# Hashed attention and a maxout feed-forward: sums gathered on 32 partitions, the last pair of a batch by halves, an earlier feed-forward and a new first pair

## The chip, the cores and the metric

The kernel runs on one core of one Trainium2 chip. The metric is the time of one execution in microseconds (us); lower is better. A core has five engines with queues of their own: PE (TensorE, matrix products into the PSUM memory; PEld is its weight load), DVE (VectorE), ACT (ScalarE), POOL (GpSimd) and SP (SyncE, which here issues transfers only). Each engine runs its instructions in the order in which the kernel emits them, and waits on semaphores for the others.

## The reference

```python
# q, k, v: (4, 8, 768, 64) fp32, proj: (64, 6); per batch and head
q_bucket, k_bucket = bits of (q @ proj > 0), bits of (k @ proj > 0)      # 6 bits each
scores = where(q_bucket == k_bucket, q @ k.T / 8, -1e9)
attn = softmax(scores);  x = attn @ v                                    # heads side by side: (3072, 512)
h = maximum(maximum(x @ w1, x @ w2), x @ w3)                             # w: (512, 768)
out = h @ w_out                                                          # (768, 512) -> (3072, 512)
```

Two tokens attend to each other only where all six signs agree. The kernel appends the six signs, as plus and minus one half, to the 64 columns of q and k, so that one matrix product of 70 rows gives the score and its mask at once; the exponential brings products with unequal signs down to nothing, and a small constant stands in for rows without a partner.

## The kernel before

Work is cut into 16 pairs of heads (four batches of four pairs) and each pair into 12 units: two halves of the queries (qh), three pairs of key blocks (kp) and two heads. A unit is one call of `scores`: two products of 70 x 384 into a double PSUM bank (tile `sc`, two buffers) and one exponential on ACT into one of 14 tiles `AT` (line 259). The loop `for u in range(NU)` (line 356, 192 units) emits everything else around the units, in an order written out by hand:

- Preparation of a pair ahead (`prep_groups`): four transpose groups (line 149, tile `mp`), each drained by DVE into `T2` (lines 152 and 154); then the hash (line 182, tile `bp`), the signs (`bits`, line 185), four small transfers `S<-bits` on SP (line 190), and casts into `S` by POOL (`even`, line 193) and DVE (`odd`, line 196). A group is emitted in four of six units until unit 61, then in two of six, and never more than six pairs ahead. Starting a pair also issues the loads of q and k two pairs further on.
- After each six units, `values`: 24 products with v (line 276) and 12 products with ones (line 283) for one half of the queries, then three DVE operations that store the unnormalized result (`avs`) and the row sums (`ys`). From pair 5 on both halves of a pair are done together, except in the very last pair.
- `normalize` of a pair: `gather` (two transfers `dd<-ys`, which spread the sums over 128 partitions), `invert` four units later (add and reciprocal on DVE, and a transfer `rd<-rr` to DRAM), `spread` six units later (two broadcast transfers `rb<-rd`), and `scale` ten units later (POOL, line 327, into `xT`). All four transfers' kinds are issued on SP.
- The feed-forward of the batch before (`ffn_groups`), from unit 13 of a batch on (`FFN_AT`): for each half of the tokens 18 groups of four products (line 213; they read all four pairs' parts of `xT`), with the maximum on DVE (lines 218 and 220), and three groups of six products with w_out (line 226), an ACT copy and a store. A credit of 0.66 per unit spaces them. Weights are loaded by POOL, 15 parts, one in three units from unit 13 (`WEIGHTS_AT`).

After the last unit the rest of batch 2's feed-forward and all of batch 3's follow, with the last normalization in between. Transposes, hashes, row sums, one of the two values tiles and the feed-forward share three PSUM buffers (`ms_ps`). The first pair has its own path (`hash_first`, lines 164 to 175): its `S` is written from PSUM by ACT, and its signs directly by DVE. Eight products with zeros run first (line 335).

Of the kernel before, what the change touches and what calls it, by code (L numbers as in the profile page):

```python
# [17 lines left out]
def kernel(  # L18
# [57 lines left out]

    iden = konst.tile([P, P], FP32, name="iden")
# [16 lines left out]
    warm = konst.tile([P, 512], FP16, name="warm")  # L94
    nc.vector.memset(warm[:], 0.0)
# [36 lines left out]
    def prep_groups(pi):  # L132
# [9 lines left out]
        def tgroup(side, hd):  # L142
            def go():
                if not st:
                    begin()
                mp = ms_ps.tile([P, 512], FP32, tag="ms", name="mp")
                n = natural[pi][side]
                for i in range(CH2):
                    nc.tensor.transpose(mp[:, i * P : (i + 1) * P], n[:, hd, 2 * i * D : (2 * i + 2) * D], iden[:])  # L149
                o = st["T2"][:, side, hd, :]  # L150
                if side == 0:
                    nc.vector.tensor_scalar(out=o, in0=mp[:, 0:HALF], scalar1=QS, scalar2=None, op0=AluOp.mult)  # L152
                else:
                    nc.vector.tensor_copy(o, mp[:, 0:HALF])  # L154
                if pi == 0:
                    for par in range(2):
                        o, i_ = st["S"][0:D, side, hd, par, :], mp[par * D : (par + 1) * D, 0:HALF]
                        if side == 0:
                            nc.scalar.mul(o, i_, QS)
                        else:  # L160
                            nc.scalar.copy(o, i_)
            return go

        def hash_first(hd):
            bp = ms_ps.tile([P, 512], FP32, tag="ms", name="bp")
            for side in (1, 0):
                for par in range(2):
                    g = 2 * side + par
                    nc.tensor.matmul(bp[32 * g : 32 * g + 32, 0:HALF], pj[:, 1 + par, :], st["T2"][:, side, hd, :],
                                     start=True, stop=True)  # L170
            for side in (1, 0):
                for par in range(2):
                    g = 2 * side + par
                    nc.vector.tensor_scalar(out=st["S"][D:KR, side, hd, par, :], in0=bp[32 * g : 32 * g + NBITS, 0:HALF],  # L174
                                            scalar1=0.0, scalar2=0.5, op0=AluOp.is_gt, op1=AluOp.subtract)

        def hashes():
# [9 lines left out]
            for hd in range(2):  # L187
                for side in (1, 0):
                    p0 = 32 * (2 * side + hd)
                    nc.sync.dma_start(st["S"][D:KR, side, hd, :, :], bits[p0 : p0 + 2 * NBITS, :])  # L190
# [7 lines left out]
        if pi == 0:  # L198
            return [tgroup(1, 0), tgroup(0, 0), lambda: hash_first(0), tgroup(1, 1), tgroup(0, 1),
                    lambda: hash_first(1)]  # L200
        return [tgroup(s, h) for h in (0, 1) for s in (1, 0)], hashes, [even, odd(1), odd(0)]

    def ffn_groups(b):
        xb = xts[b]
        gs = []
        for hf in range(2):
# [15 lines left out]
            for tb in range(CH2):  # L222
                def go2(tb=tb, hf=hf, hts=hts):
# [5 lines left out]
                    nc.scalar.copy(osb[:], ps[:, 0:DM])  # L229
                    rows = out[b * S : (b + 1) * S, :].rearrange("(p c) m -> p c m", c=NCH)  # L230
                    nc.sync.dma_start(rows[:, 2 * tb + hf, :], osb[:])
# [14 lines left out]
    WEIGHTS_AT = 13  # L246
    FFN_AT = 13
# [19 lines left out]
    def values(pi, qhs):  # L267
# [28 lines left out]
        if pi == NPAIR - 1:  # L296
            return normalize(pi, qhs[0], 1)
        return normalize(pi, 0, 2) if 1 in qhs else []

    def normalize(pi, q0, nq):  # L300
# [5 lines left out]
        W = nq * HALF // D  # L306
        dd = small.tile([P, 2, 2 * HALF // D], FP32, tag="dd", name="dd")
        rr = small.tile([P, 2 * HALF // D], FP32, tag="rr", name="rr")
        rd = drp.tile([2, 2 * HALF], FP32, tag="rd", name="rd")
# [6 lines left out]
        def invert():  # L316
            nc.vector.tensor_add(rr[:, 0:W], dd[:, 0, 0:W], dd[:, 1, 0:W])  # L317
            nc.vector.reciprocal(rr[:, 0:W], rr[:, 0:W])
            nc.sync.dma_start(rd[:, 0 : nq * HALF].rearrange("h (p i) -> h p i", i=W), rr[:, 0:W])

        def spread():
            for hd in range(2):
                nc.sync.dma_start(rb[hd * D : (hd + 1) * D, 0:nq, :],
                                    rd[hd : hd + 1, 0 : nq * HALF].to_broadcast((D, nq * HALF)))
# [5 lines left out]
        return [(0, gather), (4, invert), (6, spread)] + [(10, scale(i)) for i in range(nq)]  # L330

    with tc.manual_schedule():
        wm = ms_ps.tile([P, 512], FP32, tag="ms", name="wm")
        for _ in range(8):
            nc.tensor.matmul(wm[:], warm[:, 0:P], warm[:], start=True, stop=True)
# [5 lines left out]
        for g in first[:-1]:  # L341
# [7 lines left out]
        prep_1 = prep[3][3]  # L349
        scores(0)  # L350
        first[-1]()
        for _ in range(4):
            prep.pop(0)[2]()
        hash_ready.append(prep_1)
        cast_v[0]()
        for u in range(NU):
# [6 lines left out]
            if u >= WEIGHTS_AT and u % 3 == WEIGHTS_AT % 3 and weight_parts:  # L363
# [3 lines left out]
            if u + 1 < NU:  # L367
# [3 lines left out]
            if prep and prep[0][0] < pi + AHEAD and (u % UPG % 3 if u < UPB + FFN_AT else u % UPG in (1, 4)):  # L371
# [4 lines left out]
            elif u % UPG == 3 and u < PAIRS_AT:  # L376
# [6 lines left out]
            if u >= UPG - 1 + LAG and (u - LAG) % UPG == UPG - 1:  # L383
                vp, vq = units[u - LAG][0:2]
                single = vp * UPP < PAIRS_AT or vp == NPAIR - 1
                if single or vq == 1:
                    steps += [(u + n, g) for n, g in values(vp, (vq,) if single else (0, 1))]
                    if u >= PAIRS_AT:
# [6 lines left out]
        steps += [(1.3 * n, g) for n, g in values(NPAIR - 1, (1,))]  # L395
        steps.sort(key=lambda e: e[0])
        for n, (_, g, _) in enumerate(ffn + ffn_groups(B - 1)):
            while steps and steps[0][0] <= n:
                steps.pop(0)[1]()
            g()  # L400

# [29 lines left out]
```

## Time and profile before

| | |
|---|---|
| median of three runs | 314.0 us (313.26 to 316.84) |
| the profiled execution | 313.89 us, span 312.1 us |
| mean granted TensorE clock | 0.983 |
| busy: PE, DVE, ACT, POOL | 289.5, 193.9, 183.4, 106.3 us |
| matmuls | 2592 |
| HBM read, written | 31.46 MB, 6.39 MB |
| longest waits in total | POOL for rb 94.5 us, ACT for scores 75.5 us |

The span runs from the first to the last instruction of one execution. A line of the timeline has the start and the duration in us, the engine (SPq, ACTq, POOLq: its issue of a transfer), the line of the kernel, the operation, out<-in and the count; in brackets stands how long the engine was idle before it and what ended that. A line of waits has the total, the number of waits and the longest. Digits in the 40 slices are tenths of a slice busy; PEclk is the granted clock in tenths.

### The profile page before, as it was taken

To read this page: it belongs to the slowest core of one execution; us is meant where nothing else is said; L and a number is where in the kernel's file an instruction comes from. 1 tells how busy PE (TensorE), PEld (TensorE's weight loads), DVE (VectorE), ACT (ScalarE), POOL (GpSimd) and SP (SyncE) were. 2 spreads that over 40 slices of the span, in tenths; PEclk is the share of its full clock that TensorE was granted. 3 is DMA by queue.
4 is the path that set the end of the run, shared out by engine and by line. 5 is a ranking of instruction groups with operands and counts; after the bars stand their busy time and mean duration, and the time that the engine had idled before them with its cause. 6 is when DMAs were issued, how large, how long until landed. Compare 5 with 4: busy or idle time off the path is not lost.

```text
span 312.1 us, 6721 instructions
## 1 busy us (share of the span) xinstructions
PE 289.5 (93%) x2592; PEld 162.5 (52%) x2592; DVE 193.9 (62%) x413; ACT 183.4 (59%) x225; POOL 106.3 (34%) x125
## 2 busy tenths in 40 slices
PE   7699898988469999999999999999899999999994
PEld 3365454533236555665566555554455555555551
DVE  3868789794427755768297746762466256758480
ACT  4378777777418485755938485859585957220202
POOL 0567549394650705234140505131313020211000
PEclk9989999999959999999999999999999999999999
DMA  7758729594963324415411114022512221130202
GB/s 224 281 154 245 178 67 273 141 231 93 247 162 97 104 91 139 138 54 159 152 58 52 55 51 159 9 62 78 164 39 74 81 76 53 23 124 9 103 0 101
DMA packets 23358, 35.87 MB, mean 115 GB/s; under 512 B 9328, under 2 KB 15056, under 8 KB 23328
## 3 DMA queue, kind: packets, MB, share of 16 engines
q0 software_dynamic: 7136, 19.27, 22.3%
q1 hardware_dynamic: 16032, 16.19, 17.3%
q8 instruction: 20, 0.33, 0.4%
q14 instruction: 10, 0.08, 0.1%
q10 hardware_dynamic: 160, 0.00, 0.0%
HBM read 31.46 MB, written 6.39 MB: 121 GB/s over the span
## 4 chain that ended last, share of the span: by engine, by line
PE 70%; DMA 11%; DVE 8%; SPq 4%; ACT 3%; issue 3%; POOL 0%; DVEq 0%; ACTq 0%; POOLq 0%
PE l L213 28%; PE sc L256 14%; PE av L276 8%; PE l L226 7%; DMA dd<-ys 4%; PE sm L283 4%; DMA rb<-rd 4%; PE mp L149 4%; DMA rd<-rr 3%; ACT AT L259 3%; SPq L190 3%; PE bp L182 3%; DVE S L196 2%; DVE S L174 1%; DVE rr L317 1%
## 5 line engine op out<-in xcount | busy, mean ns | idle before, releaser
L259 ACT ACTIVATE AT<-sc,bias_t 128x768 f16<-128x768 f32 x192 | 166.7, 905 | 80.7 <-PE sc L256 75.5
L213 PE MATMUL l<-xT,w_sb 128*128 128x384 f16 x576 | 111.9, 330 | 6.7 <-POOL xT L327 6.1
L256 PE MATMUL sc<-S 70*128 70x384 bf16 x384 | 93.5, 331 | 6.1 <-ACT AT L259 4.0
L327 POOL TENSOR_TENSOR xT<-avs,rb 128x384 f16<-128x384 f32 x32 | 31.4, 998 | 142.1 <-DMA rb<-rd 94.5
L213 PEld LDWEIGHTS <-w_sb 128*128 128x128 f16 x576 | 56.4, 98 | 44.5 <-issue 9.3
L220 DVE TENSOR_TENSOR ht<-ht,l 128x384 f16<-128x384 f16 x96 | 53.2, 554 | 21.1 <-PE l L213 16.2
L256 PEld LDWEIGHTS <-S 70*128 70x128 bf16 x384 | 35.5, 99 | 43.9 <-issue 26.7
L218 DVE CAST ht<-l 128x384 f16<-128x384 f32 x48 | 26.5, 552 | 27.8 <-PE l L213 26.7
L276 PE MATMUL av<-AT,vo 128*32 128x385 f16 x768 | 37.4, 329 | 0.0
L229 ACT COPY osb<-l 128x512 f32<-128x512 f32 x24 | 14.1, 590 | 37.7 <-PE l L226 37.4
L226 PE MATMUL l<-wout_sb,ht 128*128 128x512 f16 x144 | 34.0, 379 | 0.0
L276 PEld LDWEIGHTS <-vo 128*32 128x32 f16 x768 | 18.5, 96 | 15.4 <-issue 6.7
L152 DVE TENSOR_SCALAR T<-mp 128x384 f32<-128x384 f32 x32 | 17.6, 550 | 11.3 <-PE mp L149 10.7
L193 POOL CAST S<-T 64x1536 bf16<-64x1536 f32 x15 | 22.6, 1505 | 0.9 <-DVE T L152 0.9
L196 DVE CAST S<-T 64x768 bf16<-64x768 f32 x30 | 21.8, 732 | 0.4
L226 PEld LDWEIGHTS <-ht 128*128 128x128 f16 x144 | 14.0, 97 | 14.8
L154 DVE COPY T<-mp 128x384 f32<-128x384 f32 x32 | 17.8, 556 | 6.0 <-PE mp L149 5.7
L283 PE MATMUL sm<-AT,ones 128*32 128x384 f16 x384 | 21.1, 325 | 0.0
L292 DVE TENSOR_SCALAR avs<-av,sv 128x384 f32<-128x384 f32 x32 | 19.8, 618 | 1.6
L124 POOL CAST vo<-vnat 128x768 f16<-128x768 f32 x16 | 13.4, 841 | 18.1 <-DMA vnat<-in_v_dram 16.8
L294 DVE TENSOR_SCALAR ys<-sm 128x384 f32<-128x384 f32 x32 | 17.5, 548 | 0.0
L149 PE MATMUL mp<-iden,knat 128*128 128x128 f32 x96 | 16.3, 278 | 1.2 <-DVE S L174 1.2
(36 smaller groups left out, 150.1 us busy)
## 6 DMA issues: line engine op xcount, KB each, us to landing
out_dram<-osb SPq DMA_DIRECT2D x24, 256.0 KB
vnat<-in_v_dram POOLq DMA_DIRECT2D x15, 384.0 KB, 3.6
rb<-rd SPq DMA_DIRECT2D x30, 192.0 KB
knat<-in_k_dram POOLq DMA_DIRECT2D x13, 384.0 KB, 4.3
qnat<-in_q_dram POOLq DMA_DIRECT2D x13, 384.0 KB, 4.7
w_sb<-in_moe_w_dram POOLq DMA_DIRECT2D x12, 192.0 KB, 5.0
S<-bits SPq DMA_DIRECT2D x60, 9.0 KB
knat<-in_k_dram SPq DMA_DIRECT2D x2, 384.0 KB
```

The costliest lines, as they stand in the source:

```text
L149: nc.tensor.transpose(mp[:, i * P : (i + 1) * P], n[:, hd, 2 * i * D : (2 * i + 2) * D], iden[:])
L193: nc.gpsimd.tensor_copy(st["S"][0:D, :, :, 0, :], st["T2"][0:D])
L196: return lambda: nc.vector.tensor_copy(st["S"][0:D, side, :, 1, :], st["T2"][D : 2 * D, side])
L213: nc.tensor.matmul(ps[:, 0:HALF], w_sb[wi][:, jc, fb * P : (fb + 1) * P], xb[:, jc, hf * HALF : (hf + 1) * HALF], start=(jc == 0), stop=(j ...
L218: nc.vector.tensor_copy(hts[fb][:], ps[:, 0:HALF])
L220: nc.vector.tensor_tensor(out=hts[fb][:], in0=hts[fb][:], in1=ps[:, 0:HALF], op=AluOp.max)
L226: nc.tensor.matmul(ps[:, 0:DM], hts[fb][:, tb * P : (tb + 1) * P], wout_sb[:, fb, :], start=(fb == 0), stop=(fb == NFB - 1))
L256: nc.tensor.matmul(sc[:, j, 0:HALF], th[0:KR, 1, hd, j, kp * P : (kp + 1) * P], th[0:KR, 0, hd, qh, :], start=True, stop=True)
L259: nc.scalar.activation(at[:, :, 0:HALF], sc[:, :, 0:HALF], ActFn.Exp, bias=bias_t[:], scale=SCALE)
L276: nc.tensor.matmul(av[p0 : p0 + 32, 0 : HALF + 1], vones[pi][:, hd, d0 : d0 + 32], at_of(qh, hd, c)[:, c % 2, 0 : HALF + 1], start=(c == 0 ...
L283: nc.tensor.matmul(sm[32 * t : 32 * t + 32, 0:HALF], ones[:, :], at_of(qh, hd, c)[:, c % 2, 0:HALF], start=(s == 0), stop=(s == CH2 - 1))
L327: return lambda: nc.gpsimd.tensor_mul(xt[:, jj, (q0 + i) * HALF : (q0 + i + 1) * HALF], avs[:, q0 + i, :], rb[:, i, :])
```

## The change

- Sums on 32 partitions: `dd` and `rr` have 32 rows of 48 columns (24 for a half pair), and `rd` is a DRAM tile of 32 rows that lie one behind the other. The gather is issued in `normalize` itself; for a whole pair invert comes after 5 units, spread after 8 and scale after 18 (14 for the third pair of a batch) instead of 4, 6 and 10.
- The last pair of every batch is normalized by halves, with 4, 6 and 10 units (in the last batch all at 4).
- `FFN_AT` and `WEIGHTS_AT` are 8. Weights are issued every four units instead of every three, transposes in three of six units instead of four until unit 56.
- The first pair: three of its four transposed tiles are drained by ACT, one by DVE; POOL makes its even casts, ACT (head 0) and DVE (head 1) its odd ones; hashes go into one tile for each side; the first two scores are emitted before the second head's hash; pair 1's four transpose groups go into units 0 to 3 and its hash into unit 4, half of its sign transfers on POOL. Nine warm-up products, whose tile is set first.
- The last output tile is copied by halves on ACT and DVE and stored by two queues. In the tail, steps are placed by the groups' costs rather than their number.

```diff
-                if side == 0:
+                if pi == 0 and (hd, side) != (0, 1):
+                    if side == 0:
+                        nc.scalar.mul(o, mp[:, 0:HALF], QS)
+                    else:
+                        nc.scalar.copy(o, mp[:, 0:HALF])
+                elif side == 0:
...
                 if pi == 0:
-                    for par in range(2):
-                        o, i_ = st["S"][0:D, side, hd, par, :], mp[par * D : (par + 1) * D, 0:HALF]
-                        if side == 0:
-                            nc.scalar.mul(o, i_, QS)
-                        else:
-                            nc.scalar.copy(o, i_)
+                    nc.gpsimd.tensor_copy(st["S"][0:D, side, hd, 0, :], o[0:D])
...
+        def odd_first(hd):
+            for side in (1, 0):
+                o, i_ = st["S"][0:D, side, hd, 1, :], st["T2"][D : 2 * D, side, hd, :]
+                if hd == 0:
+                    nc.scalar.copy(o, i_)
+                else:
+                    nc.vector.tensor_copy(o, i_)
...
-            return [tgroup(1, 0), tgroup(0, 0), lambda: hash_first(0), tgroup(1, 1), tgroup(0, 1),
-                    lambda: hash_first(1)]
+            return [tgroup(1, 0), tgroup(0, 0), lambda: odd_first(0), lambda: hash_first(0), lambda: bits_first(0),
+                    tgroup(1, 1), tgroup(0, 1), lambda: odd_first(1), lambda: scores(0), lambda: scores(1),
+                    lambda: hash_first(1), lambda: bits_first(1)]
...
+                    eng = nc.gpsimd if pi == 1 and hd == 1 else nc.sync
...
+                    if (b, hf, tb) == (B - 1, 1, CH2 - 1):
+                        nc.scalar.copy(osb[:, 0 : DM // 2], ps[:, 0 : DM // 2])
+                        nc.vector.tensor_copy(osb[:, DM // 2 :], ps[:, DM // 2 : DM])
+                        nc.scalar.dma_start(rows[:, 2 * tb + hf, 0 : DM // 2], osb[:, 0 : DM // 2])
+                        nc.sync.dma_start(rows[:, 2 * tb + hf, DM // 2 :], osb[:, DM // 2 :])
...
-    WEIGHTS_AT = 13
-    FFN_AT = 13
+    WEIGHTS_AT = 8
+    FFN_AT = 8
...
-        if pi == NPAIR - 1:
+        if pi % HPAIR == HPAIR - 1:
             return normalize(pi, qhs[0], 1)
...
-        W = nq * HALF // D
-        dd = small.tile([P, 2, 2 * HALF // D], FP32, tag="dd", name="dd")
-        rr = small.tile([P, 2 * HALF // D], FP32, tag="rr", name="rr")
-        rd = drp.tile([2, 2 * HALF], FP32, tag="rd", name="rd")
+        G = 16
+        W = nq * HALF // G
+        dd = small.tile([2 * G, 2, 2 * HALF // G], FP32, tag="dd", name="dd")
+        rr = small.tile([2 * G, 2 * HALF // G], FP32, tag="rr", name="rr")
+        rd = drp.tile([2 * G, W], FP32, tag=f"rd{nq}", name="rd")
...
-        return [(0, gather), (4, invert), (6, spread)] + [(10, scale(i)) for i in range(nq)]
+        gather()
+        if nq == 1:
+            return [(4, invert), (6, spread), (10, scale(0))] if pi < NPAIR - 1 else [(4, invert), (4, spread), (4, scale(0))]
+        return [(5, invert), (8, spread)] + [(18 if jj < 2 else 14, scale(i)) for i in range(nq)]
...
-        scores(0)
-        first[-1]()
-        for _ in range(4):
-            prep.pop(0)[2]()
-        hash_ready.append(prep_1)
...
-            if u >= WEIGHTS_AT and u % 3 == WEIGHTS_AT % 3 and weight_parts:
+            if u >= WEIGHTS_AT and u % 4 == WEIGHTS_AT % 4 and weight_parts:
...
-            if prep and prep[0][0] < pi + AHEAD and (u % UPG % 3 if u < UPB + FFN_AT else u % UPG in (1, 4)):
+            if prep and prep[0][0] < pi + AHEAD and (u < 4 if u < UPG else u % UPG in (0, 2, 5) if u < UPB + FFN_AT else u % UPG in (1, 4)):
...
-                single = vp * UPP < PAIRS_AT or vp == NPAIR - 1
+                single = vp * UPP < PAIRS_AT or vp % HPAIR == HPAIR - 1
```

## The prediction

> **What bounds the kernel now.** I read the page first (busy shares, the 40 slices of 7.8 us), then the chain of waits, the timelines of PE, ACT, DVE and SP in order of time, and short windows for the clock.
>
> ```profile
> PE 289.5 (93%) x2592; PEld 162.5 (52%) x2592; DVE 193.9 (62%) x413; ACT 183.4 (59%) x225; POOL 106.3 (34%) x125
> PE   7699898988469999999999999999899999999994
> PEclk9989999999959999999999999999999999999999
> ```
>
> TensorE is full from slice 13 to the last but one; PE's waits between 95 and 262 us sum to 2.1 us. There, time is TensorE work. What can be won lies in the first 93 us and the last 4. The largest hole, in PE's timeline and in windows (span, PE, PEld, DVE, ACT, POOL, clock, DMA share, GB/s):
>
> ```profile
> 81.91 0.65 PE L213 MATMUL l<-xT,w_sb 128*128 128x384 f16 x3
> 88.68 3.04 PE L213 MATMUL l<-xT,w_sb 128*128 128x384 f16 x9 [6.12 <-POOL xT L327]
> 92.15 1.23 PE L213 MATMUL l<-xT,w_sb 128*128 128x384 f16 x4
> ...
> 89.00:90.00 1.00, 1.00 (x5) 0.48 (x4) 0.56 (x1) 0.00 (x0) 1.00 (x2) 0.50 0.05 16
> 93.00:94.00 1.00, 1.00 (x7) 0.58 (x6) 0.56 (x1) 0.55 (x2) 0.66 (x1) 1.00 0.97 310
> ```
>
> The first feed-forward group has three chunks of xT and waits 6.1 us for the fourth, the last pair of batch 0. Then it runs at clock 0.50: from 88.68 to 93.22 PE does 15 matmuls that take 0.163 us each at full clock, so 4.54 us instead of 2.45. The hole costs 6.1 + 2.1 = 8.2 us. Why xT is late, from SP's timeline:
>
> ```profile
> 72.55 1.18 SPq L314 DMA_DIRECT2D dd<-ys  x2
> 76.47 0.33 SPq L319 DMA_DIRECT2D rd<-rr  x1
> 78.58 1.45 SPq L323 DMA_DIRECT2D rb<-rd  x2
> ```
>
> The gather stands behind four S<-bits issues, and the spread of 78.58 lands only at 87.5, beside 1.9 MB of vnat, knat, qnat and wout_sb that POOL issued from 76 to 81 us.
>
> Before the hole, what paces a group of six units? ACT:
>
> ```profile
> 23.10 2.48 ACT L259 ACTIVATE AT<-sc,bias_t 128x768 f16<-128x768 f32 x3 [1.01 <-PE sc L256]
> 25.79 2.48 ACT L259 ACTIVATE AT<-sc,bias_t 128x768 f16<-128x768 f32 x3 [0.21 <-PE sc L256]
> 29.35 2.48 ACT L259 ACTIVATE AT<-sc,bias_t 128x768 f16<-128x768 f32 x3 [1.08 <-PE sc L256]
> ```
>
> Six exponentials take 4.9 us; ACT starves 1.0 us behind the values block and 0.2 to 0.3 behind the hash. The values blocks start at 20.98, 27.16, 33.47, 40.74, 47.04, 54.18, 60.48, 66.79, 72.72, 79.65: groups of 5.93 (no hash), 6.3 (hash), and three of 6.9 to 7.3, where DVE stood first in a wait for the gathered sums:
>
> ```profile
> DVE rr L317 <- DMA dd<-ys: 14.1, 9, 3.2
> ```
>
> The group from 60.48 has no transposes and the one from 54.18 has four, and both take 6.3: transposes there are free, and fewer of them gain nothing.
>
> **The change, part by part.** The profiled execution took 313.89 us for a span of 312.1, so 1.8 us lie around the span; the median of the runs is 314.0. I sum on the span.
>
> *New first pair.* Before, exponentials started at 11.90, 15.51 and 16.4, and the first values block at 20.98. After, by the same rows: the warm tile is written first (0.24 us earlier), one more warm-up matmul takes 0.43, so the first transposes start at 4.7; they are drained 0.5 later by DVE (k) and ACT (q) side by side, done at 5.8. The k hash (half of 1.30 us) ends at 6.5, and four bit operations of 0.57 run from 6.55 to 8.8. Meanwhile ACT does the two odd copies (0.48 each) and POOL the two even ones (about 0.5 each, an estimate between 841 ns for 768 columns and 1505 for 1536), all by 6.9. PE's next transposes wait for a ms buffer until 7.7, scores(0) waits for the third bit operation until 8.3, and the first two exponentials start at 8.7 and 9.5. For head 1, DVE has two casts and four bit operations from 8.8 on; scores(3) starts at 11.3. Then four evacuations for pair 1 (0.55 each) end at 14.0, its hash at 14.7, and the first values block starts at 16.0. That is 5.0 us earlier. Bounds: 1.5 us earlier, if each of seven handoffs costs 0.25 more and PE is at clock 0.5 for 3.3 us (1.65 lost); 6 us earlier, if POOL and the ms ring never hold PE. The clock row is this:
>
> ```profile
> 13.00:14.00 1.00, 0.32 (x3) 0.31 (x3) 0.97 (x2) 0.00 (x0) 0.00 (x0) 1.00 0.73 286
> 15.00:16.00 1.00, 1.00 (x5) 0.57 (x4) 0.52 (x2) 0.49 (x1) 1.00 (x3) 0.50 0.15 32
> ```
>
> The clock fell at 14.2 us though PE had worked in every microsecond before. The Trainium skill, "TensorE: Matmul & The Clock Gate", the section on the HAM clock gate, says that it falls after an idle window of about 3.4 us; by that rule neither kernel would slow in its start, and the lower bound would be 1.65 us better. I go by the row for the bound. For the sum I take no slow stretch, since PE works some 5.5 of the 7 us from 5 to 12, more than before.
>
> Pair 1's bits go half by POOL: two issues of 0.75 us, with POOL's even cast and the loads of pair 4 queued behind them. They land by about 20.4 at the row of the slow loads (3.6 us); its scores come at 21. Cover gone, PE waits about 1 us.
>
> *Sums on 32 partitions, other delays.* A gather has 32 pieces of 192 bytes for 128 of 48. Landing is unknown: bounded by the chain's 1.96 and 3.80 us for dd, 2.09 and 4.70 for rd; I take 2. DVE's add and reciprocal have 48 columns for 12: 171 and 224 ns before, at most some 0.3 us more each, seventeen times on a DVE that is 62% busy: nothing. The gather goes out at the same place; invert comes a unit (1.0 us) later, scale four to eight units later, so POOL's 94.5 us of waiting for rb no longer holds its loads. The 32-row store gives the same contiguous read back. What goes is the DVE wait of the long groups, except for the last pair, where invert stays at four units: I charge 1.0 us in all. Hashes fall into five of the eight groups from unit 6 to 54: 5 x 6.3 + 3 x 5.93 + 1.0 = 50.3, against 51.74 (20.98 to 72.72): 1.4 us gained; bounds 4.3 gained (all at 5.93) and 1.5 lost (two long groups stay).
>
> *Feed-forward from unit 8, transposes spread.* After the values block of unit 54 (then 66.3), PE has 1.6 us of values and two scores with ACT's wait: the first feed-forward matmul comes at 69.3, 3.0 us later, against 9.2 before (72.72 to 81.91). But work left out of that stretch comes later, on a full PE: ten score matmuls (1.63), a values block (1.6), three hashes at 0.65 (1.95), eight transpose groups at 0.33 (2.65), together 7.8. So 10.8 against 9.2: 1.6 lost.
>
> *Last pair by halves.* The first feed-forward groups read half 0 alone. Its values come at unit 42, invert 46, spread 48, scale 52. On SP the spread stands behind the second half's gather, which waits for ys of unit 48: ys near 63.3, spread issued until 65.7, landed by 68.6 (3.27 us in the chain), scaled at 69.6; the fourth matmul needs it at 69.8. The last w3 chunk goes out at unit 52, behind two scales on POOL, near 65.1, lands 3.8 to 6.1 us later, and is needed at 71.0. Both just fit: I charge 0.5 of the 8.2, so 7.7 gained. Bounds: all 8.2 gained, or none. Three more normalizations in the kernel are 15 SP issues (0.34 to 0.55 us) that lie beside the full PE.
>
> *Last output tile by halves.* The copy of 0.58 us (from 307.96) becomes about 0.3, and the 3.6 us from its end to the end of the span keep the same bytes in flight: 0.3 gained, bounds 0 and 0.8. The Trainium skill, "DMA: Bandwidth & Descriptors", section on the anatomy of one DMA, puts some 2 us of a transfer that POOL issues down to a fixed cost; were it so for SP's and ACT's, which no run here shows, the halves would gain next to nothing beside the copy.
>
> Sum: 312.1 - 5.0 - 1.4 + 1.6 - 7.7 - 0.3 = 299.3 span, and 301.1 us with the 1.8 around it.
>
> **The rivals.**
>
> *The hole only moves.* Unit 56 comes at 69 us with its rb and w3 just landed; if the spread takes the 8.4 us that it took from 78.58, xT comes at 74.6, PE waits 5 us and runs slow after it. For it: that row, and the new place behind the second gather. Against: half the bytes, and 1.3 MB of loads at units 47 and 48 for 1.9. 301.1 + 7.7 = 308.8.
>
> *The start gains little* (its lower bound): 301.1 + 3.5 = 304.6; with the long groups kept too, 304.6 + 2.9 = 307.5. For it: a ring of three ms buffers, shared by transposes and hashes of both heads. Against: the two engines that drain them run side by side.
>
> *Slower.* The feed-forward of every batch now starts five units earlier, with the same scales. In batches 1 and 2 xT's half 0 is scaled at unit 4 and read at unit 8: four units of some 1.7 us, 6.7 us of cover. If SP (output stores, bits, the second half's gather before the first half's spread) delays that spread by more, PE waits at each of three starts; at a lateness of 8.2 us, with the slow clock, it pays three times: 301.1 - 0.5 + 24.6 = 325. It decides from a lateness of 4.3 us beyond the cover at each of the three (301.1 + 3 x 4.3 = 314). For it: POOL's longest wait for rb is 12.9 us. Against: that wait begins when POOL is idle, and PE met no wait over 0.8 us there.
>
> *It gains more*: groups at 5.93 and no charge for the first feed-forward: 301.1 - 2.9 - 0.5 = 297.7.
>
> **How the numbers follow.** Forecast (298.5 to 305) 0.62; little gained at the start 0.13; hole moved 0.12; more gained 0.08; slower 0.05. The time is the forecast's, 301.1. The range is 296.5 to 308.5: it takes in the cases up to the moved hole, about half of whose chance lies above it, and leaves out that, the slower case and the far ends of the bounds. About 1% (3.1 us) is what a measurement of this kernel can tell, its runs reaching from 313.3 to 316.8. Faster by more than that: 0.92, within it 0.04, slower 0.04 (the slower case near its point of decision counts as the same).
>
> **What would show each step.** First exponential near 8.7 and first values block near 16; values block of unit 54 near 66; no PE wait for xT over 1 us and no clock of 0.50 after the start; transposes and hashes still running on PE past 150 us; L317 no longer waiting over 1.5 us; PE full from 70 us to the end. A PE wait for w_sb or xT of over 3 us near 70 us, a values block at 19 us, or a second hole at a batch's unit 8 would prove a step wrong.

## The result, and the profile after

The changed kernel takes 324.7 us (median of four runs, 321.7 to 325.4) against 313.6 (310.6 to 316.8) for the kernel before in the same rounds: 1.037 times as long, 95% interval 1.026 to 1.048. The forecast was 301.1, so it is wrong, and in its sign. The profiled execution took 324.5 us for a span of 322.8, at a mean granted clock of 0.974.

From here on, medians, ratios and differences leave out the slow executions, those over 1.5% above the fastest of the same kernel in its block (ranges, and the times that the recorded expectations quote, are of all runs), and little more than waits is read from the profiles of e2_delays, e5_first_pair and e14_late_ffn8, which are of such executions. The experiments ran in four blocks, each with its own runs of the kernel before: medians 313.7, 313.8, 309.4 (a single run) and 313.2 us, single runs from 309 to 321. So differences of 2 or 3 us between blocks say little.

The span splits at four events that can be read in PE's timeline:

| stretch, us | before | forecast | after | after less forecast |
|---|---|---|---|---|
| to the first values block | 20.98 | 16.0 | 17.64 | +1.6 |
| from there to the values block of unit 54 | 51.74 | 50.3 | 57.93 | +7.6 |
| from there to the first feed-forward matmul | 9.19 | 3.0 | 3.58 | +0.6 |
| from there to the end | 230.2 | 230.0 | 243.6 | +13.6 |
| span | 312.1 | 299.3 | 322.8 | +23.5 |

The page after, busy time with the slices of 8.1 us:

```profile
PE 297.6 (92%) x2593; PEld 165.3 (51%) x2593; DVE 201.8 (63%) x419; ACT 183.0 (57%) x222; POOL 109.1 (34%) x131
...
PE   8889989888999999996999999996999999979995
...
PEclk9998979997999999999999999999899999979999
```

The deep hole of 4 and 6 tenths in slices 11 and 12 is gone. In its place come dips in slices 19, 28 and 36, which are the starts of the feed-forward of batches 1 and 2 and of the tail, and dips of the clock in slices 4, 6, 10, 29 and 36. PE is busy 8.1 us longer with the same products (and one more warm-up), and idle 2.6 us longer. Half clock explains at most 3.1 of the 8.1: by the mean clocks it cost 8.4 us of the span after and 5.3 of the span before. Where the rest comes from is not shown. Whether the half clock is a cause or only follows from thin work is left to the experiments. The feed-forward's starts, in PE's timeline:

```profile
80.92 1.62 PE L226 MATMUL l<-xT,w_sb 128*128 128x384 f16 x9 [1.11 <-POOL xT L347]
...
152.55 1.62 PE L226 MATMUL l<-xT,w_sb 128*128 128x384 f16 x9 [1.60 <-POOL xT L347]
...
224.43 2.42 PE L226 MATMUL l<-xT,w_sb 128*128 128x384 f16 x9 [1.69 <-POOL xT L347]
...
286.12 4.12 PE L226 MATMUL l<-xT,w_sb 128*128 128x384 f16 x14 [2.31 <-POOL xT L347]
```

Line 226 is what line 213 was. The wait of 6.12 us at the first start is now 1.11, but there are four waits instead of one, 6.7 us in all, and behind the last two the matmuls run long: nine of them took 1.62 us at 152 and 2.42 at 224.

In the attention stage, ACT's timeline:

```profile
34.24 2.48 ACT L278 ACTIVATE AT<-sc,bias_t 128x768 f16<-128x768 f32 x3 [1.40 <-PE sc L275]
37.69 2.49 ACT L278 ACTIVATE AT<-sc,bias_t 128x768 f16<-128x768 f32 x3 [0.96 <-PE sc L275]
41.58 4.29 ACT L278 ACTIVATE AT<-sc,bias_t 128x768 f16<-128x768 f32 x5 [1.40 <-PE sc L275]
...
49.32 2.48 ACT L278 ACTIVATE AT<-sc,bias_t 128x768 f16<-128x768 f32 x3 [2.17 <-PE sc L275]
```

Behind a values block ACT now starves 1.40 us instead of 1.0 to 1.08: a transpose group of 0.33 us stands between the scores and the values block of the same unit. DVE and POOL, side by side in time:

```profile
111.70 3.43 DVE L337 TENSOR_TENSOR rr<-dd 32x48 f32<-32x48 f32 x1
112.10 0.84 POOL L124 CAST vo<-vnat 128x768 f16<-128x768 f32 x1
...
113.58 1.48 POOL L205 CAST S<-T 64x1536 bf16<-64x1536 f32 x1
115.16 0.44 DVE L338 RECIPROCAL rr<-rr 32x48 f32<-32x48 f32 x1
...
116.06 0.81 PE L226 MATMUL l<-xT,w_sb 128*128 128x384 f16 x4 [0.43 <-DVE ht L231]
```

An addition of 48 columns, with a median of 0.19 us, took 3.43 and ended when POOL's second cast did; three more took 1.92. DVE's feed-forward copies stand behind it, and PE behind them. Last, two lines of the waits (total, times, longest):

```profile
DVE rr L337 <- DMA dd<-ys: 12.4, 6, 4.1
...
PE l L226 <- POOL xT L347: 6.7, 4, 2.3
```

DVE still stands in order before gathered sums; that was to have gone. And SP, around the last pair of batch 0:

```profile
71.35 0.55 SPq L339 DMA_DIRECT2D rd<-rr  x1
72.00 1.21 SPq L334 DMA_DIRECT2D dd<-ys  x2
76.35 1.15 SPq L343 DMA_DIRECT2D rb<-rd  x2
```

The first half's spread goes out at 76.35, where the prediction had it issued by 65.7. The stage itself is 9.3 us late by then (75.57 against 66.3 at unit 54), so the steps hold their order and most of the lateness comes from ahead of them.

### The profile page after: what moved, and what is told of

Same layout as the page of the kernel before. It is cut to its first block, busy times and chain, and to the rows that moved or that the text cites. A ratio compares the mean times of both kernels' runs of the same rounds, so it can differ in the third digit from the quotient of the medians.

```text
span 322.8 us, 6762 instructions
## 1 busy us (share of the span) xinstructions
PE 297.6 (92%) x2593; PEld 165.3 (51%) x2593; DVE 201.8 (63%) x419; ACT 183.0 (57%) x222; POOL 109.1 (34%) x131
## 2 busy tenths in 40 slices
DMA packets 19491, 35.88 MB, mean 111 GB/s; under 512 B 4960, under 2 KB 11700, under 8 KB 19460
## 4 chain that ended last, share of the span: by engine, by line
PE 71%; DMA 8%; DVE 7%; ACT 5%; issue 3%; SPq 3%; POOL 2%; POOLq 0%; ACTq 0%; DVEq 0%
PE l L226 28%; PE sc L275 15%; PE av L295 9%; PE l L239 6%; ACT AT L278 5%; PE mp L149 5%; PE sm L302 4%; DMA rb<-rd 4%; DVE rr L337 3%; PE bp L193 3%; DMA rd<-rr 3%; DMA dd<-ys 2%; SPq L202 2%; POOL xT L347 2%; PE wm L358 1%
## 5 line engine op out<-in xcount | busy, mean ns | idle before, releaser
L226 PE MATMUL l<-xT,w_sb 128*128 128x384 f16 x576 | 114.2, 332 | 8.8 <-POOL xT L347 6.7
L275 PE MATMUL sc<-S 70*128 70x384 bf16 x384 | 91.1, 329 | 9.5 <-ACT AT L278 9.1
L233 DVE TENSOR_TENSOR ht<-ht,l 128x384 f16<-128x384 f16 x96 | 53.1, 553 | 19.9 <-PE l L226 15.2
L295 PE MATMUL av<-AT,vo 128*32 128x385 f16 x768 | 39.8, 343 | 0.0
L205 POOL CAST S<-T 64x1536 bf16<-64x1536 f32 x15 | 22.2, 1478 | 21.2 <-DVE T L157 21.2
L295 PEld LDWEIGHTS <-vo 128*32 128x32 f16 x768 | 18.9, 99 | 16.6 <-issue 8.5
L302 PE MATMUL sm<-AT,ones 128*32 128x384 f16 x384 | 22.1, 337 | 0.0
L159 DVE COPY T<-mp 128x384 f32<-128x384 f32 x31 | 17.0, 549 | 7.4 <-PE mp L149 6.3
L157 DVE TENSOR_SCALAR T<-mp 128x384 f32<-128x384 f32 x30 | 16.5, 550 | 7.9 <-PE mp L149 6.8
L337 DVE TENSOR_TENSOR rr<-dd 32x48 f32<-32x48 f32 (+1 forms) x20 | 13.5, 676 | 12.5 <-DMA dd<-ys 12.4
L208 DVE CAST S<-T 64x768 bf16<-64x768 f32 x30 | 17.6, 599 | 0.7
L310 DVE TENSOR_SCALAR sv<-av 128x1 f32<-128x1 f32 x32 | 4.9, 154 | 20.0 <-PE av L295 19.6
```

The source lines that it names most:

```text
L205: nc.gpsimd.tensor_copy(st["S"][0:D, :, :, 0, :], st["T2"][0:D])
L226: nc.tensor.matmul(ps[:, 0:HALF], w_sb[wi][:, jc, fb * P : (fb + 1) * P], xb[:, jc, hf * HALF : (hf + 1) * HALF], start=(jc == 0), stop=(j ...
L233: nc.vector.tensor_tensor(out=hts[fb][:], in0=hts[fb][:], in1=ps[:, 0:HALF], op=AluOp.max)
L275: nc.tensor.matmul(sc[:, j, 0:HALF], th[0:KR, 1, hd, j, kp * P : (kp + 1) * P], th[0:KR, 0, hd, qh, :], start=True, stop=True)
L295: nc.tensor.matmul(av[p0 : p0 + 32, 0 : HALF + 1], vones[pi][:, hd, d0 : d0 + 32], at_of(qh, hd, c)[:, c % 2, 0 : HALF + 1], start=(c == 0 ...
L302: nc.tensor.matmul(sm[32 * t : 32 * t + 32, 0:HALF], ones[:, :], at_of(qh, hd, c)[:, c % 2, 0:HALF], start=(s == 0), stop=(s == CH2 - 1))
```

## The experiments

Three suspects came out of this: the new places of the transposes, the new delays of the normalization, and the feed-forward from unit 8. The first three runs undo one each.

**Transposes in four of six units again** (e1_transposes4)

```diff
-            if prep and prep[0][0] < pi + AHEAD and (u < 4 if u < UPG else u % UPG in (0, 2, 5) if u < UPB + FFN_AT else u % UPG in (1, 4)):
+            if prep and prep[0][0] < pi + AHEAD and (u < 4 if u < UPG else u % UPG % 3 if u < UPB + FFN_AT else u % UPG in (1, 4)):
```

> The changed kernel with one thing undone: transposes in four of six units until unit 56, as before, instead of three. Theory T (the spread of the transposes): one of the three groups stands right ahead of the values block, so ACT starves 1.40 us there instead of 1.07, and PE, with less work, falls to clock 0.50 in three stretches between 20 and 80 us. By T the values block of unit 54 comes back from 75.6 to 68 to 70 us, no clock of 0.50 is left between 20 and 75 us, eight fewer transpose groups lie on the full PE, and the span falls from 322.8 to 314 or 315. Theory N (the normalization's new delays let DVE's add meet POOL's work) and theory F (the earlier feed-forward meets xT late at every batch) both expect less than 2 us from this edit.

312.9 us (311.5 to 321.3), 0.996 times the kernel before (0.990 to 1.002): 11.8 us below the changed kernel. The direction held, the place did not: unit 54 came at 76.8 us, because one group took 12.5 us behind a wait of DVE for sums and an addition of 1.89 us, with 6.8 us at half clock behind it. The whole gain lies behind the first feed-forward matmul. This is the stretch from there to the end, in the changed kernel and here (span, PE, PEld, DVE, ACT, POOL, clock, DMA share, GB/s):

```profile
79.15:322.76 243.61, 228.40 (x1983) 130.09 (x1980) 153.71 (x303) 132.74 (x160) 65.40 (x71) 0.99 0.30 88
79.06:309.34 230.28, 220.59 (x1946) 125.82 (x1943) 140.23 (x290) 132.41 (x160) 58.15 (x65) 1.00 0.28 86
```

At that matmul the changed kernel had done 33 of its 64 transpose groups, this run 40 (the kernel before 41). PE has 7.8 us less work behind it and 5.5 us less idle time, and no stretch at half clock is left there.

**Delays 4, 6 and 10 again** (e2_delays)

```diff
-        return [(5, invert), (8, spread)] + [(18 if jj < 2 else 14, scale(i)) for i in range(nq)]
+        return [(4, invert), (6, spread)] + [(10, scale(i)) for i in range(nq)]
```

> The changed kernel with the delays of whole pairs as before (invert 4, spread 6, scale 10 units). Theory N: the adds of 1.92 and 3.43 us at 95, 112, 131 and 168 us come back to 0.2 us, and with each PE gets back 1 to 2.5 us, so 5 to 8 us in all. Theory T: less than 2 us. Theory F: xT is no earlier for the last pair, so the waits at the batch starts stay, less than 2 us.

321.8 us from one run of four (321.8 to 331.4): the 5 to 8 us that theory N forecast are not seen, though the additions did get shorter (1.30 us at most). Whether the time changed at all cannot be told. In its profile DVE's waits for dd doubled to 24.9 us, with 4.58, 8.39 and 5.22 before the first three additions, which began 7 to 9 us after the gather's first issue (25.75 and 32.84, 44.02 and 53.06, 62.18 and 69.90). In the changed kernel the first three, which waited too, began 5.3 to 5.6 us after it. So the suspicion had the wrong sign: shorter delays mean longer waits, and the new delays are still too short.

**Feed-forward from unit 13 again** (e3_ffn13)

```diff
-    FFN_AT = 8
+    FFN_AT = 13
```

> The changed kernel with the feed-forward from unit 13 as before. Theory F: the four waits for xT (6.7 us) and the clock of 0.50 behind two of them (some 3 us) go, and five units of feed-forward come back to the tail (3.3 us, less what PE did not use there), so the span falls by 5 to 7 us to 316 to 318. Theory T and theory N: a gain of less than 2 us, or a loss of up to 3.3 us, as the earlier feed-forward filled PE.

311.8 us (311.5 to 313.5), 0.988 (0.982 to 0.994): 12.9 us below the changed kernel. No wait for xT is left at any start, and no addition took over 1.0 us. So the early start costs more than its visible waits; DVE's additions also meet POOL's casts less often without it. The edit does one thing more: the constant also sets the unit up to which three groups of transposes are emitted in six units (56 there, 61 here), so that 37 of the 64 were done at the first feed-forward matmul.

**The new first pair alone, in the kernel before** (e5_first_pair)

> The kernel before with the new first pair alone (its order, its engines, nine warm-up products, pair 1's transposes in units 0 to 3). If the start is worth what the traces show at the first values block (17.6 for 21.0 us), the span falls from 312.1 to 308 to 309.5. The rival: ACT or the hole at 82 us takes the gain back, as the same loads and normalizations end no earlier, and the span stays at 311 to 313.

313.5 us (312.2 to 329.3), 1.006 (0.995 to 1.018), no difference that can be told. In its profile the first values block came at 17.26 us, 3.7 earlier, and then DVE waited 22.2 us in all for dd (4.09 and 4.85 before the first two sums): a gather issued at 44.1 was added at 52.5. So the earlier start shows in no median; the waits are where it can have been lost.

The next block asks how each loss works.

**The sum over one operand** (e9_one_input)

```diff
-            nc.vector.tensor_add(rr[:, 0:W], dd[:, 0, 0:W], dd[:, 1, 0:W])
+            nc.vector.tensor_reduce(out=rr[:, 0:W], in_=dd[:, :, 0:W].rearrange("p h w -> p w h"),
+                                    op=AluOp.add, axis=mybir.AxisListType.X)
```

> The changed kernel with the sum of the two halves of dd made as a reduction over one operand instead of an addition of two. Theory P (an addition with two SBUF inputs is held up while POOL casts): the additions of 1.92, 3.43, 1.92 and 1.92 us fall below 0.6 us; PE's waits behind them (0.76 and 0.43 us the largest) go, and the time is 1 to 4 us below the changed kernel's 324.7. Rival (the length comes from a late transfer or semaphore): the reductions last as long, and the time is unchanged.

320.3 us (317.4 to 323.9), 1.024 (1.016 to 1.032). All instructions of that line (durations in ns, shortest, median, longest):

```profile
L337 DVE TENSOR_REDUCE rr<-dd x20: 182/235/246, 34.3 to 284.5; 32x48 f32<-32x96 f32 x12, 32x24 f32<-32x48 f32 x8
```

The longest is 0.25 us instead of 3.43, while POOL casts as before: the length came from the two operands. By the medians it was worth 4.4 us, but the interval overlaps that of the changed kernel (1.026 to 1.048), so that its size is uncertain.

**Idle products to keep PE busy** (e13_idle_products)

```diff
+        if 8 < u < UPB + FFN_AT and (u - 1) % UPG in (1, 4):
+            for j in range(2):
+                for _ in range(3):
+                    nc.tensor.matmul(sc[:, j, HALF:512], warm[:, 0:P], warm[:, 0:P], start=True, stop=True)
```

> The changed kernel with six products of zeros (128 columns each, about 0.32 us together) after the scores in two of the six units that have no transposes, from unit 9 to 56; they write columns that nobody reads. Theory C (the half clock of the attention stage, three stretches of 3.41 us, comes from PE having too little to do, and costs the pace): these stretches go, unit 54's values block comes at 70 to 73 us instead of 75.6, and the time is 3 to 5 us below 324.7. Rival S (the pace is lost to waits of ACT and DVE, and the clock only follows): the clock may rise, the values blocks come where they came or later, and the time is within 2 us of the changed kernel's.

323.8 us (321.3 to 324.6), 1.023 (1.016 to 1.030).

```profile
PEclk9999999999999999999999999998999999979999
...
ACT AT L282 <- PE sc L280: 16.6, 14, 1.7
```

The clock is full up to slice 27, and yet the eight groups from the first values block to unit 54 took 57.8 us (16.41 to 74.18) against 57.9. Theory C's gain is not there, as rival S expected. The run alone does not settle it: 14 waits of ACT, 16.6 us, now end at the idle products (line 280), so they may have cost what the clock gave.

**Three transposes, away from the values block** (e1b_transposes3_early)

```diff
-            if prep and prep[0][0] < pi + AHEAD and (u < 4 if u < UPG else u % UPG in (0, 2, 5) if u < UPB + FFN_AT else u % UPG in (1, 4)):
+            if prep and prep[0][0] < pi + AHEAD and (u < 4 if u < UPG else u % UPG in (1, 2, 4) if u < UPB + FFN_AT else u % UPG in (1, 4)):
```

> The changed kernel with the same number of transposes, three in six units, but in the second, third and fifth unit of a group instead of the first, third and last: none next to the values block. Theory P (a transpose group between scores and the values block keeps ACT waiting 0.33 us longer in each of eight groups): ACT's wait behind the values block is 1.07 us again instead of 1.40, unit 54's values block comes at 70 to 73 us instead of 75.6, and the time is 319 to 322. Rival A (what was lost is PE's activity or the number of transposes): the time is within 1.5 us of the changed kernel's 324.7.

319.3 us (315.8 to 322.7). Its ACT timeline:

```profile
39.40 4.86 ACT L278 ACTIVATE AT<-sc,bias_t 128x768 f16<-128x768 f32 x6 [1.07 <-PE sc L275]
45.33 2.69 ACT L278 ACTIVATE AT<-sc,bias_t 128x768 f16<-128x768 f32 x3 [1.07 <-PE sc L275]
```

The 1.40 is 1.07 again, unit 54 comes at 70.4 us (53.1 from the first values block instead of 57.9), and the same number of transposes costs 5.4 us less for the place alone. The clock is full in this stage (0.998 in the mean) as in e13_idle_products with its 57.8 us, so the pace differs at the same clock. From the first feed-forward matmul to the end it takes 241.0 us, not 230.3 as in e1_transposes4: the place mends the attention stage, the fourth group what comes behind it.

**Two parts undone, then later inversions too** (e11_t4_ffn13, e12_late_invert). The second adds to the first:

```diff
-            return [(4, invert), (6, spread), (10, scale(0))] if pi < NPAIR - 1 else [(4, invert), (4, spread), (4, scale(0))]
-        return [(5, invert), (8, spread)] + [(18 if jj < 2 else 14, scale(i)) for i in range(nq)]
+            return [(7, invert), (9, spread), (12, scale(0))] if pi < NPAIR - 1 else [(4, invert), (4, spread), (4, scale(0))]
+        return [(8, invert), (10, spread)] + [(18 if jj < 2 else 14, scale(i)) for i in range(nq)]
```

> The changed kernel with two parts undone together: transposes in four of six units and the feed-forward from unit 13. Alone these gave 314.9 and 311.8 us. If the two losses are separate, they add: about 302. If both are the same loss (DVE and POOL colliding, xT late), 309 to 312. Whole pairs' sums are still inverted five units after their gather, so the stall that both had near 60 to 70 us (DVE waiting 2.4 to 3.5 us for dd) should still stand, worth 4 to 5 us.

> The kernel of e11_t4_ffn13 with the sums inverted later: 8 units after the gather for a whole pair (spread 10), 7 for a half (spread 9, scale 12). Theory D (DVE stands in order before gathered sums that land 5 us after their issue): DVE's waits for dd fall from about 11 us in all to under 3, unit 54's values block comes near 69 instead of near 76, no half clock after 20 us, and the time is 4 to 6 us below that of e11_t4_ffn13. Rival (the loads fill the queues, so the stall moves to rb or to S): the same time within 1.5 us, with waits for rb, xT or S in place of those for dd.

e11 took 309.3 us (307.3 to 317.6), 0.978 (0.968 to 0.987): the two losses overlap, and the stall near 60 to 70 us still stands (a group of 11.9 us). e11 differs from e1_transposes4 in the feed-forward's start alone, so that beside four groups of transposes in six units the early start costs 3.6 us, not 12.9. e12 took 303.8 us (302.1 to 305.1), 0.961 (0.955 to 0.967): the later inversion is worth 5.5 us in this kernel. Its page:

```profile
PE 287.1 (95%) x2593; PEld 161.6 (54%) x2593; DVE 197.2 (65%) x419; ACT 181.9 (60%) x222; POOL 109.1 (36%) x131
...
PEclk9999999999999999999999999999999999999998
```

No slice but the last has a low clock, though nothing was done for it, and the groups from the first values block to unit 54 take 52.0 us. The expectation of dd waits under 3 us missed (7.1 left).

**Feed-forward from unit 8 in that kernel** (e14_late_ffn8; e12 with `FFN_AT = 8` and a half's delays of 4, 6, 10, which it needs)

> The kernel of e12_late_invert with the feed-forward and the weights from unit 8 again, and the halves of a batch's last pair with the changed kernel's 4, 6 and 10 units, which that needs. e12_late_invert took 303.8 us. Theory F (the feed-forward's start meets xT late in every batch whatever the attention stage does, and the work left out comes back later): 9 to 13 us more, 313 to 317, with three or four waits of PE for xT of 1 to 2.3 us. Rival (the early feed-forward was bad only because DVE and POOL were late with the sums): within 3 us of e12_late_invert, and no such waits.

315.5 us from two runs of four (313.3 to 322.3), 11.7 more. A line of its waits (total, times, longest):

```profile
PE l L226 <- POOL xT L347: 10.1, 3, 5.4
```

Theory F holds: with the sums inverted later too, the early start meets xT late, by 5.4 us at the longest where 2.3 was expected. **Later inversions alone in the changed kernel** (e18_after_late):

> The changed kernel with its whole pairs' sums inverted 8 units after the gather and spread after 10, instead of 5 and 8, and nothing else. Theory D (DVE stands before sums that land late, so inverting later is worth the 6.2 us that it was worth with the two other parts undone): DVE's waits for dd fall from 12.4 us to under 6, and the time is 318 to 320. Rival (here the late starts of the feed-forward and the transposes next to the values block decide, and hide it): within 2 us of 324.7.

324.1 us (323.0 to 324.8), 1.032 (1.023 to 1.041). DVE's dd waits fell from 12.4 to 6.4 us, and the attention stage from 57.9 to 54.9 us, but PE's waits for xT grew from 6.7 to 10.7, so the rival is right here: later sums help only where the feed-forward does not read them at once.

**The halves of the last pair alone, in the kernel before** (e6_halves), **and with later inversions** (e17_before_halves_late)

> The kernel before with one part of the change alone: the last pair of every batch is normalized by halves, with the old delays, the old gather over 128 partitions and the feed-forward from unit 13. Theory H (as in the prediction: the hole of 6.1 us at the first feed-forward matmuls and the 2.1 us of half clock behind it go): no wait of PE for xT over 1 us near 85 us, and the time is 6 to 8 us below the kernel before. Rival (the hole moves to the second spread, or to w_sb): within 3 us of the kernel before.

319.7 us (318.2 to 321.5), where the kernel before took 309.4 to 318.4 in this block and has medians of 313.2 to 313.8 in the others: not 8 us faster but some 6 slower. PE's wait for xT did go, but DVE's waits for dd grew from 14.1 to 33.3 us. DVE and SP, in order of time:

```profile
63.84 0.38 SPq L319 DMA_DIRECT2D rd<-rr  x1
...
69.29 1.15 SPq L323 DMA_DIRECT2D rb<-rd  x2
70.53 1.22 SPq L314 DMA_DIRECT2D dd<-ys  x2
...
74.10 0.17 DVE L317 TENSOR_TENSOR rr<-dd 128x6 f32<-128x6 f32 x1 [7.31 <-DMA dd<-ys]
```

In the kernel before, a due spread is issued ahead of a new gather. The spread of pair 2 went out 5.4 us after its rd, the gather of the first half stood behind it, and DVE had been standing in the addition since 66.8, before that gather was even issued. The change issues the gather inside `normalize`, ahead of what is due.

> The kernel of e6_halves (319.7 us) with later inversions: 8, 10 and 14 units for a whole pair, 7, 9 and 12 for a half. Theory D (e6_halves lost because the spread of pair 2, which stands on SP ahead of the first half's gather, held that gather and with it DVE by 7.3 us): the waits of 7.3 and 8.0 us of DVE for dd go, the hole at the first feed-forward matmuls too, and the time is 305 to 309. Rival (halves cost something else, two more normalizations per batch on SP, or loads in the way): 313 or more.

314.3 us (311.1 to 317.0), 1.002 (0.997 to 1.008): 5 us back, and the 7.3 and 8.0 are gone, the wait for xT is 2.0 us, but no gain on the kernel before. Theory D was half right; something else was missing.

**The gather on 128 partitions again** (e16_gather128), **beside its base** (e15_late_one_input, which is e12 with the sum over one operand)

> The kernel of e12_late_invert (303.8 us) with the sum of the two halves of dd as a reduction over one operand. There the longest addition took 0.94 us; all should now be below 0.3 us. If the additions still held up DVE's evacuations, 0.5 to 1.5 us are gained; if other work covers them, the same time within 0.7 us.

> The kernel of e15_late_one_input (302.4 us) with the sums gathered over 128 partitions and stored as in the kernel before. As in the prediction (the gather's shape is worth nothing): 302.4 within 1.5 us. Theory G (32 longer rows land sooner than 128 short pieces): 2 to 5 us more, with waits of DVE for dd above the 5.8 us in all of e15_late_one_input. Rival: the addition and reciprocal of 12 columns instead of 48 free DVE, and it is faster by 0.5 to 2 us.

e15 took 302.4 us (301.2 to 303.4) against 309.4 to 318.4 for the kernel before in its block, faster than both kernels and the fastest of all here; on e12 its 1.4 us are within what two blocks can tell. e16, with the old `dd`, `rr`, `rd`, gather and spread, took 311.0 (307.3 to 313.5), 0.987 (0.981 to 0.993): 8.5 us more for a part that I had priced at nothing. Between the two profiles lie 10.3 us, 3.5 of them in the attention stage and 5.9 behind the first feed-forward matmul. e15's SP (the stores of the first and the second half's sums) and PE at the first feed-forward:

```profile
68.08 0.34 SPq L339 DMA_DIRECT2D rd<-rr  x1
...
73.76 0.53 SPq L339 DMA_DIRECT2D rd<-rr  x1
...
77.31 1.62 PE L226 MATMUL l<-xT,w_sb 128*128 128x384 f16 x9 [0.43 <-POOL xT L347]
```

and e16's:

```profile
73.81 3.60 SPq L338 DMA_DIRECT2D rd<-rr  x1
...
83.00 0.60 SPq L338 DMA_DIRECT2D rd<-rr  x1
...
86.19 3.04 PE L226 MATMUL l<-xT,w_sb 128*128 128x384 f16 x9 [4.88 <-POOL xT L346]
```

With 25139 packets instead of 19491, SP's issue of the first half's rd takes 3.60 us instead of 0.34 while the loads run, bits and spread stand behind it, and the hole of the kernel before is back, 4.88 us and half clock (3.04 us for nine matmuls) behind it. Theory G's 2 to 5 us are exceeded. DVE's dd waits grew from 5.8 to 8.5 us only, so part of the way is SP; how the loss divides is not shown.

## Why the prediction was wrong

Of the 23.5 us that the span lies above the sum, 13.6 come behind the first feed-forward matmul, 7.6 in the attention stage before it, and 1.6 at the start.

*New first pair, -5.0.* Measured -3.3. The first exponential came at 9.81 instead of 8.7. The mis-sized term is DVE's: its first bit operation began at 7.45 instead of 6.55, and the two casts for head 1 beside POOL's took 1.70 us. The 3.3 us only count if the next stage keeps them; in e5_first_pair no gain was left (313.5 against 313.7 us). For the sum I took no slow stretch in the start, and none came before 23.7 us. (In the kernel before the clock fell at 14.48 us, not at 14.2: its window from 14.00 to 15.00 has 0.74.)

*Attention stage, -1.4.* Measured +6.2. The step that failed is "transposes there are free, and fewer of them gain nothing". I had compared two groups of the kernel before by their number of transposes and never looked at where in the unit a group would land. A group ahead of the values block costs ACT 0.33 us eight times, and e1b_transposes3_early shows 4.8 us of the stage gone with the place alone. "Fewer of them gain nothing" was wrong in sign as well: e1_transposes4 shows 13.3 us gone behind the first feed-forward matmul with the fourth group, where the sum had charged 4.6 us for eight groups and three hashes. The second failed term is the 1.0 us charged for DVE's waits, and behind it the landing of 2 us that I took. One unit more before the inversion does not cover sums that land 5.3 to 5.6 us after their issue, as the first three did. Three units more shorten the changed kernel's stage by 3.1 us (e18_after_late), which with the 4.8 covers the 7.6 by which the stage missed the forecast. The time of the changed kernel does not follow, that of the kernel with two parts undone does, by 5.5 us (e12_late_invert).

*"At most some 0.3 us more each ... nothing"* for the addition. Measured up to 3.43 us, and some 4 us of the time by medians whose intervals overlap (e9_one_input). The Trainium skill, "GPSIMD Engine Reference", section Specifications, says that POOL shares its SBUF interfaces with VectorE and that they contend where a DVE instruction has two SBUF inputs. The runs agree: up to 3.43 us with two, at most 0.25 with one. I had the row of 856 ns for the longest addition of the kernel before and took the median.

*Feed-forward from unit 8, +1.6.* Undoing it gave 12.9 us in the changed kernel (with some transposes moved as well), 11.7 with four groups in six units and later sums (e14 against e12, two runs), but 3.6 with four groups and the changed kernel's delays (e1 against e11). So beside the changed kernel's delays the early start and the transposes left for behind it cost together what neither costs alone; with later sums the early start is dear again. The sum counted only the work that moves, 7.8 us; it left the cover out. PE's idle time there, which was to fall by the hole, rose by 2.6 us, and its busy time by 10.8 (217.6 us before). This is the rival I gave 5 in 100, with 325 us as its time and 324.7 measured. The agreement is partly luck: its lateness of 8.2 us at each of three starts was in truth 1.1 to 2.3 us at four, and placement, inversion, the transposes left for later and the addition made up the rest. The argument against it, "that wait begins when POOL is idle", was no argument: POOL idle says that the sums are the last thing to come, which is the rival's very condition.

*Last pair by halves, -7.7.* In the changed kernel the hole did go, from 6.12 to 1.11 us, as the step said. But the halves do not bring time by that alone. In the kernel before they remove the hole too and cost some 6 us by DVE's waits ahead of it (e6_halves), with later sums nothing is won (e17_before_halves_late), and with the gather on 128 partitions, which I had put at nothing, the hole is back (4.88 us in e16). The step priced the parts one by one, though the halves, the inversion and the gather act on one chain. No run takes the halves out of e15, so what they are worth there is not shown.

*Last tile, -0.3.* From the start of the last copy to the end of the span it is 4.1 us before and 3.9 after: 0.2, as good as foreseen.

What the forecast had right is the room. With the transposes, the inversion, the feed-forward's start and the addition mended, e15's span is 299.1 us (its fastest run), close to the 299.3 that I summed, though with other terms.

What stays open: how much of the early feed-forward's loss is its waits, how much the transposes left for behind it, and how much the collisions of DVE and POOL that it brings; I ran it neither with the sum over one operand and four groups, nor with later sums at equal half delays.

## What to carry to other kernels

Before a stage is called free, put each moved instruction at its place between two others and ask who starves behind it: the same three transposes cost 5.4 us more in one place than in another. Price parts of a change that feed one chain (gather, inversion, spread, scale, first reader) together, with the landing time of the slowest load-laden moment: the halves lost time alone and stand in the fastest kernel here. For an engine that waits in order for a small late transfer, try a later instruction (5.5 us in e12_late_invert), but see who reads the result: where the feed-forward read it at once, it won nothing (e18_after_late).

## What the runs showed of the hardware

DVE's addition with two SBUF operands can be held while POOL works. In the changed kernel the additions of 1.92, 3.43, 1.92 and 1.92 us each ended 0.07 us after one of POOL's casts; as a reduction over one operand none took over 0.25 us. Not every meeting holds it: this one, and one at 203.26, met a cast and took 0.20 and 0.19 us.

```profile
184.56 0.20 DVE L337 TENSOR_TENSOR rr<-dd 32x48 f32<-32x48 f32 x1
184.60 1.49 POOL L205 CAST S<-T 64x1536 bf16<-64x1536 f32 x1 [4.81 <-DVE T L157]
```

The granted clock falls for stretches of 3.41 us, and it falls without an idle stretch. Windows of the changed kernel, set to where half clock begins and ends (span, PE, PEld, DVE, ACT, POOL, clock, DMA share, GB/s):

```profile
20.31:23.72 3.41, 2.46 (x15) 1.42 (x13) 1.95 (x3) 3.41 (x6) 3.41 (x6) 1.00 0.60 195
23.72:27.13 3.41, 3.41 (x39) 1.38 (x38) 1.42 (x4) 0.91 (x2) 3.41 (x5) 0.50 1.03 238
64.68:68.09 3.41, 2.39 (x15) 0.92 (x14) 2.01 (x6) 1.16 (x2) 2.13 (x3) 1.00 0.03 5
68.09:71.51 3.42, 3.23 (x48) 2.03 (x48) 3.35 (x8) 2.02 (x4) 2.15 (x3) 1.00 0.95 221
...
221.69:225.11 3.42, 1.65 (x10) 0.90 (x10) 0.32 (x1) 1.61 (x3) 1.72 (x2) 1.00 0.56 203
225.11:228.52 3.41, 3.41 (x12) 1.59 (x11) 1.35 (x3) 0.90 (x1) 0.35 (x2) 0.50 0.16 58
```

After 2.46 us of PE work in a window the clock fell, after 2.39 it held. Ahead of the kernel's other stretches at half clock (from 44.20, 74.92 and 286.55) PE worked 2.40, 2.40 and 1.11 us of 3.41. So PE needs no idle window to lose its clock, a thin one can do, and the busy time of the window alone does not decide. The rule of an idle window, which the prediction quoted from the Trainium skill ("TensorE: Matmul & The Clock Gate", the section on the HAM clock gate), asks for more than these runs do.

The issue of the same small transfer on SP can take several times as long while loads run: 0.34 us for the first half's rd in e15 and 3.60 in e16. What decides is not shown. The number of pieces does not do it alone, for in the kernel before, with 23358 packets, no issue of rd took over 0.52 us.
